# Output products with 32 weight columns instead of 4, and the result stored in two transfers instead of four

## The chip, the cores and the metric

The kernel runs on one core of a Trainium2 chip. The metric is the device time in microseconds (us). The kernel before takes 662.51 us (median of three runs, 662.46 to 662.76).

## The reference

One decoding step of a transformer block for four batch rows of width 640. From the normalised input `xn`, an attention branch over a cache and a gated MLP branch are computed, and both are added to the input:

```python
x = A_x
xn = _layernorm(x, axis=-1)
return x + _A_ref(xn, A_k_cache, A_v_cache, A_wq, A_wo) + _B_ref(xn, B_w_in, B_w_sp, B_b_sp, B_w_out)
```

The attention has 32 heads of 128 elements and 4096 cached positions for each of the four batch rows, one query each. Its two caches are 134 MB each, in bf16:

```python
q = (x @ wq).reshape(B, Sq, Hq, Dh).transpose(0, 2, 1, 3)
scores = jnp.einsum('bhqd,bhkd->bhqk', q, k) * Dh ** (-0.5)
p = _softmax(scores, axis=-1)
o = jnp.einsum('bhqk,bhkd->bhqd', p, v)
return o.transpose(0, 2, 1, 3).reshape(B, Sq, Hq * Dh) @ wo
```

The MLP multiplies `xn` by `w_in` (640 by 1728), applies gelu, normalises one half, scales and shifts it, multiplies it with the other half and multiplies by `w_out` (864 by 640).

## The kernel before

The work is cut into 16 steps: four groups of eight heads, and the four batches of each. A step loads 8 MB of keys into one of two `k_nat` buffers (L139) and 8 MB of values into the single buffer of the pool `vp` (L145); a row of each load is 64 KB in one partition. Nearly all loads are issued by SP, one after the other, in the order that the code gives: MLP and query weights, keys 0 and 1, and from there values and keys by turns. The first tenant of the value buffer is `w_sb`, which holds the MLP weights, and its last is `wo`, the attention's output weights (5.1 MB). These are loaded by four transfers in SP's queue (L159), issued when step 14's values have been used; the last two bring row blocks 11 to 14 and 15 of the second half. The values of step 15 go into a key buffer (`v_last`).

For each step VectorE multiplies the keys by the query (L449), folds the halves (L463), TensorE sums (L475), VectorE reduces (L486) and finds maxima (L495, L505), ScalarE takes the exponentials (L542), VectorE spreads them over the heads (L553), and TensorE weights the values (L568). ScalarE takes the sums out of PSUM (L578), and a small matmul (L591) picks out each head's own row. The schedule is manual: PE, DVE, ACT and SP run in the order in which the code is written; GpSimd (POOL) has constants to make and nothing more (L167 to L176, L232 to L259, L305).

**Output products.** The result is collected in one PSUM tile, `out_ps`, of 128 partitions by 160 columns. `add_out` (L214 to L222) issues four matmuls, one for each quarter q of the 640 output columns; quarter q goes to the partitions from 32q on, in four strips of 32. The moving operand has 160 columns of a weight matrix. The stationary operand holds the four batches, so it has four columns, and the batches stand in lanes 32q to 32q + 3. Only the first call (L224), which adds the input, has 32 columns. There are 12 calls in the MLP, from `yT` (L405) and `yE` (L416), and 32 in the attention (`group_proj`, L653), from two tiles `oT0` and `oT1` of 128 by 16 by 4 that `group_turn` writes (L650, L651): the first half after step 8, the second at the very end. At the end TensorE runs `group_proj(0)`, `group_turn(1)`, `group_proj(1)`; ScalarE copies `out_ps` into `res` (L732); and four transfers of four lanes by 320 bytes each store it (L736), two issued by SP and two by ACT.

Of the kernel before, what the change touches and what calls it, by code (L numbers as in the profile page):

```python
# [10 lines left out]
BF16 = mybir.dt.bfloat16  # L11
ACT = mybir.ActivationFunctionType
ALU = mybir.AluOpType
# [4 lines left out]
def kernel(  # L18
# [39 lines left out]
    GW = P // CG  # L58
    ROWS = HT * Bsz
    NG = 2  # L60
    HP = HG // NG
    WH = NG * HT
    WL = P // WH
    WJ = WH * Dh // P
    WW = 2
    WR = NG * ROWS
    NFF = Fh // P
    TL = 16
    TK = (Fh - NFF * P) // TL
    TE = 4  # L70
    NFC = NFF + TK
    F0 = NFF * P
    TF = TL * TK
    NZ = NFF + 1
    assert F0 + TF == Fh and TF <= P
    NQ = 4
    NO = D // NQ
    REP = GW // Bsz
    assert CB * HT == GW and ROWS == GW

    const = ctx.enter_context(tc.tile_pool(name="const", bufs=1))
    kp = ctx.enter_context(tc.tile_pool(name="kp", bufs=2))
    vp = ctx.enter_context(tc.tile_pool(name="vp", bufs=1))
    work = ctx.enter_context(tc.tile_pool(name="work", bufs=1))
# [12 lines left out]
    def v_slot(name):  # L97
        return vp.tile([P, SLOT], BF16, tag="v", name=name)
# [3 lines left out]
    x_bf = start_t[:Bsz, 0:D]  # L102
# [3 lines left out]
    w_sb = v_slot("w_sb")  # L106
    w_in_sb = w_sb[:, 0 : DC * F].rearrange("p (c n) -> p c n", c=DC)
    w_out_sb = w_sb[:, DC * F : DC * F + NFC * D].rearrange("p (k n) -> p k n", k=NFC)
    nc.sync.dma_start(
        out=w_out_sb[:, 0:NFF, :], in_=B_w_out[0 : NFF * P].rearrange("(p k) n -> p k n", k=NFF)  # L110
    )
# [10 lines left out]
    for l in range(TL // TE):  # L122
        nc.sync.dma_start(
            out=w_out_sb[:TL, NFF:NFC, :].rearrange("(e l) k n -> e l (k n)", e=TE)[:, l],
            in_=B_w_out[F0:Fh].rearrange("(e l k) n -> e l (k n)", e=TE, k=TK)[:, l],
# [25 lines left out]
    wo_t = []  # L151
    WO_CUTS = ((0, WJ), (0, 11, 15, WJ))

    def load_wo():
        t = v_slot("wo")[:, 0 : HP * WJ * D].rearrange("p (g j n) -> p g j n", g=HP, n=D)
        wo_t.append(t)
        for g in range(HP):
            for j0, j1 in zip(WO_CUTS[g], WO_CUTS[g][1:]):
                nc.sync.dma_start(out=t[:, g, j0:j1, :], in_=wo_v[g][:, j0:j1, :])  # L159
# [4 lines left out]
    ident = const.tile([P, P], BF16)  # L164
# [17 lines left out]
    for i in range(NSTAT):  # L182
# [5 lines left out]
        out=rstd[:], in_=mv[:, 1:2], func=ACT.Sqrt, bias=eps_tile[:Bsz], scale=1.0  # L188
# [3 lines left out]
        out=xn_bf,  # L192
        in0=x_bf,
# [8 lines left out]
    for c in range(DC):  # L202
        nc.tensor.transpose(
            out=xnT_ps[:, c, :], in_=xn_v[:, c, :], identity=ident[:Bsz, :Bsz]
# [3 lines left out]
        out=xnT_r[:], in_=xnT_ps[:, :, :, None].to_broadcast([P, DC, Bsz, REP])  # L208
# [5 lines left out]
    def add_out(lhsT, rhs, start=False, stop=False):  # L214
        for q in range(NQ):
            nc.tensor.matmul(  # L216
                out=out_ps[GW * q : GW * q + lhsT.shape[1], :],
                lhsT=lhsT,
                rhs=rhs[:, q * NO : (q + 1) * NO],
                start=start,  # L220
                stop=stop,
            )  # L222

    add_out(ident[:Bsz, :GW], x_bf, start=True)  # L224


    own = const.tile([P, HT], FP32)
# [1 line left out]
        out=own[:], in_=ident_f[:].rearrange("p (h l) -> p h l", h=HT), axis=AX.X, op=ALU.add  # L229
# [4 lines left out]
        out=pick[:, :, GW - HT : GW],  # L234
        in_=ident_f[:].rearrange("p (j h c) -> p c h j", c=CB, h=HT),
        axis=AX.X,
        op=ALU.add,
# [3 lines left out]
        out=row_head_f[:],  # L241
        in_=ident_f[:WR, :WR].rearrange("p (g b h) -> p g h b", g=NG, h=HT),
        axis=AX.X,
        op=ALU.add,
# [3 lines left out]
        out=row_head[:],  # L248
        in_=row_head_f[:].rearrange("p g h -> p (g h)")[:, :, None].to_broadcast([WR, WH, WL]),
# [3 lines left out]
        out=row_batch_f[:],  # L253
        in_=ident_f[:WR, :WR].rearrange("p (g b h) -> p b g h", g=NG, h=HT),
        axis=AX.XY,
        op=ALU.add,
# [10 lines left out]
    for t in range(2):  # L267
        for c in range(DC):
            for j in range(CG):
                n = CG * t + j  # L270
                nc.tensor.matmul(  # L271
                    out=q_ps[t][GW * j : GW * (j + 1), :],
                    lhsT=xnT_r[:, c].rearrange("p b r -> p (b r)"),
                    rhs=wq_t[:, c, n * NW : (n + 1) * NW],
                    start=(c == 0),
# [3 lines left out]
    for t in range(2):  # L279
        qT_ps = ps_m.tile([P, HQ, CG, Bsz, REP], BF16, tag="m", name="qT_ps")  # L280
        for n in range(HQ):
            nc.tensor.transpose(  # L282
                out=qT_ps[:, n].rearrange("p j b r -> p (j b r)"),
                in_=q_rows[:, t, n * Dh : (n + 1) * Dh],
# [3 lines left out]
            out=qT[:, CG * HQ * t : CG * HQ * (t + 1), :].rearrange(  # L288
                "p (j n) b -> p n j b", n=HQ
            ),  # L290
            in_=qT_ps[:, :, :, :, 0],
# [17 lines left out]
    def gmlp():  # L309
        zz, gw, gt, gz, sq = (gm[n] for n in ("zz", "gw", "gt", "gz", "sq"))  # L310
# [30 lines left out]
        for n, src in enumerate((gz[:, 1, :, :], sq)):  # L341
# [51 lines left out]
            out=sq,  # L393
# [7 lines left out]
            in1=ac_sb[:, None, Bsz : 2 * Bsz].to_broadcast([P, NZ, Bsz]),  # L401
            op=ALU.add,
        )
        yT = work.tile([P, NZ, Bsz], BF16, name="yT")
        nc.vector.tensor_tensor(out=yT[:], in0=gz[:, 0, :, :], in1=sq, op=ALU.mult)  # L405
        ye_ps = ps_m.tile([TL, TK, Bsz], FP32, tag="m", name="ye_ps")
        for k in range(TK):
            nc.tensor.matmul(
                out=ye_ps[:, k, :],
                lhsT=ident[:TF, :TF].rearrange("p (f k) -> p k f", k=TK)[:, k, :],  # L410
                rhs=yT[:TF, NFF, :],
                start=True,
                stop=True,
            )
        yE = work.tile([TL, TK, Bsz], BF16, name="yE")
        nc.scalar.copy(out=yE[:], in_=ye_ps[:])  # L416
        for k in range(NFC):
            if k < NFF:
                add_out(yT[:, k], w_out_sb[:, k, :])
            else:  # L420
                add_out(yE[:, k - NFF], w_out_sb[:TL, k, :])


    qbcs, scores, sums_ps, maxes, pms, pvs, es = {}, {}, {}, {}, {}, {}, {}
# [58 lines left out]
    def row_sums(i, u):  # L483
        if u == 0:
            scores[i] = small.tile([P, NC], FP32, name="s_sb", bufs=1)
        nc.vector.tensor_reduce(  # L486
            out=scores[i][:, u * UC : (u + 1) * UC],
            in_=sums_ps[i][:],
            axis=AX.X,
            op=ALU.add,  # L490
        )
# [146 lines left out]
    def group_turn(g):  # L638
        parts = oTs[g]
        JW = WJ // WW  # L640
        t_ps = ps_m.tile([P, WJ, Bsz], FP32, tag="m", name="t_ps")
        for j in range(WJ):
            nc.tensor.matmul(
                out=t_ps[:, j, :],
                lhsT=parts[j // JW][:, j % JW, :, :],
                rhs=row_batch[:],
                start=True,
                stop=True,
            )
        oTs[g] = const.tile([P, WJ, Bsz], BF16, name=f"oT{g}")  # L650
        nc.scalar.copy(out=oTs[g][:], in_=t_ps[:])  # L651

    def group_proj(hg):  # L653
        for j in range(WJ):
            add_out(
                oTs[hg][:, j, :],
                wo_t[0][:, hg, j, :],
                stop=(hg == HP - 1 and j == WJ - 1),
            )
# [14 lines left out]
    with tc.manual_schedule(engines={E.PE, E.DVE, E.Activation, E.SP}):  # L674
        stage_q(0)
        gmlp()
        load_v(0, v_slot("v_nat"))
        for i in range(NT):
            product(i, 0)
            at(i - 1, row_sums, 1)  # L680
            at(i - 1, lane_max)
            at(i - 1, turn_max)
            at(i - 1, head_max)
            at(i - 1, spread_max)
            fold(i, 0)
            joined(i - 2, group_rows)
            sums(i, 0)
            joined(i - 2, group_turn)
            at(i - 1, bias)
            at(i - 1, exps)  # L690
            at(i + 1, stage_q)
            at(i - 1, own_heads)
            at(i - 1, weighted)
            if i == 0:
                pass
            elif i < NT - 1:
                load_v(i, v_slot("v_nat"))
            else:
                load_wo()
            at(i - 1, take)  # L700
            product(i, 1)
            row_sums(i, 0)
            fold(i, 1)
            at(i - 1, diag)
            group(i - 1, group_den)
            sums(i, 1)
            if i + 2 < NT:
                load_k(i + 2)
            elif i + 2 == NT:
                load_v(NT - 1, k_slot("v_last"))  # L710
        L = NT - 1
        row_sums(L, 1)
        lane_max(L)
        joined(L - 1, group_rows)
        turn_max(L)
        head_max(L)
        spread_max(L)
        bias(L)
        exps(L)
        own_heads(L)  # L720
        for c0, c1 in zip(V_CUTS, V_CUTS[1:]):
            weighted(L, c0, c1)
        take(L)
        group_den(HG - 1)
        diag(L)
        group_rows(HP - 1)
        group_proj(0)
        group_turn(HP - 1)
        group_proj(HP - 1)

        res = small.tile([P, NO], BF16, tag="s_sb", name="res", bufs=1)
        nc.scalar.copy(out=res[:], in_=out_ps[:])  # L732
        out_v = out.flatten_outer_dims()
        for q in range(NQ):
            queue = nc.scalar if q % 2 else nc.sync
            queue.dma_start(  # L736
                out=out_v[:, q * NO : (q + 1) * NO], in_=res[GW * q : GW * q + Bsz]
            )


# [28 lines left out]
```

## Time and profile before

| | |
|---|---|
| median of three runs | 662.51 us (662.46 to 662.76) |
| profiled execution, first to last instruction | 661.1 us |
| bytes read | 282.24 MB, 427 GB/s over the span |
| busy: VectorE (DVE) | 491.6 us (74%) |
| busy: TensorE matmul (PE) / weight load (PEld) | 295.4 us (45%) / 127.9 us (19%) |
| busy: ScalarE (ACT) / GpSimd (POOL) | 34.4 us (5%) / 2.1 us |
| granted TensorE clock, mean | 0.712 |

The profile shows one execution. Its time is the span from the first to the last instruction; the runs' time also counts what lies around the span, some 1.4 us here. Engines have the names in brackets, SP issues transfers, and a q behind a name means its instruction queue (ACTq, SPq). A group of instructions is named by its line in the kernel, what it writes and what it reads; "128*4 128x160" is a matmul with 128 rows and 4 weight columns that writes 128 by 160 elements as the profile counts them. An entry "[0.62 <-DMA wo]" says how long the engine had been idle before and what ended it.

### The profile page before, as it was taken

How to read it: one execution, taken by the hardware profiler on the slowest of the kernel's cores; microseconds unless marked ns; L12 is line 12 of the kernel's file. 1: busy time of each engine (PE TensorE's matmuls, PEld its weight loads, DVE VectorE, ACT ScalarE, POOL GpSimd, SP SyncE). 2: the span in 40 equal slices, each digit the busy share in tenths (PEclk: the TensorE clock that was granted, in tenths of full speed). 3: DMA queues.
4: the chain of work that ended last, by engine and by line, in shares of the span. 5: the costliest groups of instructions: out<-in, count | busy, mean ns of one | idle time of the engine just before them, and what ended most of it. 6: DMA issues, size and time to landing. Idle time of an engine off the chain costs nothing.

```text
span 661.1 us, 4720 instructions
## 1 busy us (share of the span) xinstructions
PE 295.4 (45%) x2099; PEld 127.9 (19%) x2099; DVE 491.6 (74%) x222; ACT 34.4 (5%) x94; POOL 2.1 (0%) x15
## 2 busy tenths in 40 slices
PE   0513464536426253552625344362634507263656
PEld 0301121212112021220202112120211202031223
DVE  1249999959597795959779569986959699695851
ACT  0300000000000000000000000000000000000000
POOL 1000000000000000000000000000000000000000
PEclk9756676876858687675868757787775768777688
DMA  8999999999999999999999999999999999999996
GB/s 377 456 428 444 428 417 441 429 436 441 436 420 433 432 429 445 440 421 432 424 436 441 440 425 432 420 441 436 437 428 437 425 432 429 440 432 437 432 406 275
DMA packets 5712, 282.55 MB, mean 427 GB/s; under 512 B 680, under 2 KB 812, under 8 KB 1084
## 3 DMA queue, kind: packets, MB, share of 16 engines
q1 hardware_dynamic: 5664, 282.24, 98.9%
q8 instruction: 16, 0.26, 0.2%
q14 instruction: 4, 0.03, 0.0%
q10 hardware_dynamic: 28, 0.01, 0.0%
HBM read 282.24 MB, written 0.01 MB: 427 GB/s over the span
## 4 chain that ended last, share of the span: by engine, by line
DMA 51%; DVE 37%; PE 9%; issue 2%; ACT 1%; SPq 0%; DVEq 0%; ACTq 0%
DMA k_nat<-in_A_k_cache_dram 47%; DVE k_nat L449 22%; DVE k_nat L463 11%; PE s_ps L475 8%; DMA wo<-in_A_wo_dram 4%; DVE s_sb L486 3%; DMA w_sb<-in_B_w_out_dram 1%; ACT p L542 1%; PE pv L568 1%; DVE m L495 1%; PE mT L500 0%; DVE nm L505 0%; DVE pm L553 0%; SPq L159 0%; PE out_ps L216 0%
## 5 line engine op out<-in xcount | busy, mean ns | idle before, releaser
L449 DVE TENSOR_TENSOR k_nat<-k_nat,qbc 128x16384 bf16<-128x16384 bf16 x32 | 278.0, 8688 | 97.8 <-DMA k_nat<-in_A_k_cache_dram 97.8
L475 PE MATMUL s_ps<-k_nat,ident 128*128 128x512 bf16 x528 | 184.8, 528 | 139.3 <-DVE k_nat L463 139.3
L463 DVE TENSOR_TENSOR k_nat<-k_nat 128x8192 bf16<-128x8192 bf16 x31 | 136.7, 4410 | 0.0
L475 PEld LDWEIGHTS <-ident 128*128 128x128 bf16 x528 | 65.3, 129 | 248.3 <-DVE k_nat L463 123.3
L500 PE MATMUL mT<-ident_f,m 128*1 128x128 f32 x16 | 5.9, 366 | 160.0 <-DVE m L495 160.0
L568 PE MATMUL pv<-v_nat,pm 128*32 128x512 bf16 x960 | 56.1, 387 | 0.8 <-DVE pm L553 0.8
L486 DVE TENSOR_REDUCE s_sb<-s_ps 128x128 f32<-128x1024 f32 x32 | 39.0, 1218 | 5.4 <-PE s_ps L475 5.4
L500 PEld LDWEIGHTS mT<-ident_f,m 128*1 128x1 f32 x16 | 1.3, 79 | 167.8 <-DVE m L495 156.2
L568 PEld LDWEIGHTS <-pm 128*32 128x32 bf16 x1024 | 27.1, 100 | 34.3 <-issue 8.5
L553 DVE TENSOR_TENSOR pm<-p,own_c 128x2048 bf16<-128x2048 bf16 x16 | 19.6, 1225 | 15.3 <-ACT p L542 15.3
L542 ACT ACTIVATE p<-s_sb,nb 128x256 bf16<-128x256 f32 x16 | 8.1, 508 | 394.1 <-DVE nb_h L524 394.1
L591 PE MATMUL o_ps<-e,pick 128*32 128x128 f32 x128 | 17.0, 276 | 11.2 <-ACT e L578 11.2
L591 PEld LDWEIGHTS o_ps<-e,pick 128*32 128x32 f32 x128 | 12.7, 109 | 18.7 <-ACT e L578 18.7
L578 ACT COPY e<-pv 128x512 f32<-128x512 f32 x16 | 9.4, 586 | 68.1 <-PE pv L568 60.6
L287 DVE COPY qT<-qT_ps 128x64 bf16<-128x64 bf16 x2 | 0.4, 224 | 15.5 <-PE qT_ps L282 15.5
L516 PE MATMUL nb_ps<-nm,ones_row 1*128 1x8 f32 x32 | 9.2, 359 | 6.0 <-DVE nm L505 6.0
L505 DVE TENSOR_REDUCE nm<-mT 1x8 f32<-1x128 f32 x16 | 4.5, 279 | 7.5 <-PE mT L500 7.5
L516 PEld LDWEIGHTS nb_ps<-nm,ones_row 1*128 1x128 f32 x32 | 7.7, 298 | 10.6 <-DVE nm L505 9.9
L271 PE MATMUL q_ps<-wq,xnT_r 128*32 128x512 bf16 x40 | 4.3, 609 | 11.2 <-DMA wq<-in_A_wq_dram 11.2
L443 ACT CAST qbc<-qbc_ps 128x128 bf16<-128x128 f32 x16 | 4.3, 266 | 92.3 <-PE qbc_ps L435 92.3
L608 PE MATMUL den<-ones_col,acc_h 128*32 128x1 f32 x8 | 1.0, 194 | 16.6 <-DVE acc_h L601 16.6
L495 DVE TENSOR_REDUCE m<-s_sb 128x1 f32<-128x256 f32 x16 | 6.7, 420 | 0.5
(92 smaller groups left out, 70.7 us busy)
## 6 DMA issues: line engine op xcount, KB each, us to landing
wq<-in_A_wq_dram SPq DMA_DIRECT2D x1, 5120.0 KB, 16.3
wo<-in_A_wo_dram SPq DMA_DIRECT2D x1, 2560.0 KB
w_sb<-in_B_w_in_dram SPq DMA_DIRECT2D x1, 2160.0 KB, 20.9
wo<-in_A_wo_dram SPq DMA_DIRECT2D x1, 1760.0 KB
w_sb<-in_B_w_out_dram SPq DMA_DIRECT2D x1, 960.0 KB
wo<-in_A_wo_dram SPq DMA_DIRECT2D x1, 640.0 KB, 25.5
k_nat<-in_A_k_cache_dram SPq DMA_DIRECT2D x16, 39.6
v_nat<-in_A_v_cache_dram SPq DMA_DIRECT2D x15, 33.7
```

Source lines behind the costliest of these rows:

```text
L449: nc.vector.tensor_tensor(out=part(i, u), in0=part(i, u), in1=qbcs[i][:, None, :].to_broadcast([P, UC, Dh]), op=ALU.mult,)
L463: nc.vector.tensor_tensor(out=t[:, :, 0:HD2], in0=t[:, :, 0:HD2], in1=t[:, :, HD2:Dh], op=ALU.add)
L475: nc.tensor.matmul(out=sums_ps[i][:, c : c + SC], lhsT=ident[:], rhs=t[:, c : c + SC, g * RW : (g + 1) * RW], start=(g == 0), stop=(g == n ...
L486: nc.vector.tensor_reduce(out=scores[i][:, u * UC : (u + 1) * UC], in_=sums_ps[i][:], axis=AX.X, op=ALU.add,)
L495: nc.vector.tensor_reduce(out=m1[:], in_=scores[i][:], axis=AX.X, op=ALU.max)
L500: nc.tensor.transpose(out=mT[:], in_=maxes[i][:], identity=ident_f[:])
L516: nc.tensor.matmul(out=nb_ps[:], lhsT=ones_row[:], rhs=maxes[i][:], start=True, stop=True)
L542: nc.scalar.activation(out=probs[i][:], in_=scores.pop(i)[:], func=ACT.Exp, bias=maxes.pop(i)[:], scale=scale_qk, accum_out=accs[hg][:, b ...
L553: nc.vector.tensor_tensor(out=pm[:], in0=probs.pop(i)[:] .rearrange("p (n c) -> p n c", c=CB)[:, :, None, :] .to_broadcast([P, NB, HT, CB] ...
L568: nc.tensor.matmul(out=pvs[i][j * GW : (j + 1) * GW, :], lhsT=pm[:, n, :, :].rearrange("p h c -> p (h c)"), rhs=v_nat[:, n * CB : (n + 1) ...
L578: nc.scalar.copy(out=es[i][:], in_=pvs.pop(i)[:].rearrange("p (c d) -> p c d", d=Dh))
L591: nc.tensor.matmul(out=o_ps[hg // NG][own_rows(hg), :], lhsT=pick[:, c, GW - HT - HT * b : 2 * GW - HT - HT * b], rhs=e[:, c, :], start=(b ...
```

## The change

The stationary operand of every output product gets 32 columns: batch b stands in column 8b (`REP` is 8), and the seven columns behind it are zero. So the results stand in lanes 32q + 8b, and each of the two transfers at the end takes the eight lanes of two quarters, one issued by ACT and one by SP. Three places provide the zeroed room. `x_rep` is a new constant of four by 32 elements. `y_rep` lies behind the MLP weights in `w_sb`; `o_rep` lies behind the output weights in `wo`, 1024 elements a partition. GpSimd zeroes both. The results are then written into every eighth column: `yT` by VectorE, `yE` by ScalarE, the second half of the attention by ScalarE straight from PSUM. The first half still goes to `oT0` after step 8, since the room in `wo` isn't there yet, and a new copy, `group_rep`, brings it over after the last turn of the loop, ahead of the last step's exponentials on ACT.

```diff
+    y_at = DC * F + NFC * D
+    y_rep = w_sb[:, y_at : y_at + (NZ + TK) * GW].rearrange(
+        "p (k b r) -> p k b r", b=Bsz, r=REP
+    )
+    yT, yE = y_rep[:, 0:NZ], y_rep[:TL, NZ : NZ + TK]
...
     def load_wo():
-        t = v_slot("wo")[:, 0 : HP * WJ * D].rearrange("p (g j n) -> p g j n", g=HP, n=D)
+        w = v_slot("wo")
+        t = w[:, 0 : HP * WJ * D].rearrange("p (g j n) -> p g j n", g=HP, n=D)
         wo_t.append(t)
+        o_rep = w[:, HP * WJ * D : HP * WJ * (D + GW)]
+        nc.gpsimd.memset(o_rep, 0.0)
+        wo_t.append(o_rep.rearrange("p (g j b r) -> p g j b r", g=HP, b=Bsz, r=REP))
...
-    add_out(ident[:Bsz, :GW], x_bf, start=True)
+    x_rep = const.tile([Bsz, Bsz, REP], BF16)
+    nc.gpsimd.tensor_copy(
+        out=x_rep[:], in_=ident[:Bsz, :Bsz, None].to_broadcast([Bsz, Bsz, REP])
+    )
+    nc.gpsimd.memset(w_sb[:, y_at : y_at + (NZ + TK) * GW], 0.0)
+    add_out(x_rep[:].rearrange("c b r -> c (b r)"), x_bf, start=True)
...
-        yT = work.tile([P, NZ, Bsz], BF16, name="yT")
-        nc.vector.tensor_tensor(out=yT[:], in0=gz[:, 0, :, :], in1=sq, op=ALU.mult)
+        nc.vector.tensor_tensor(
+            out=yT[:, :, :, 0], in0=gz[:, 0, :, :], in1=sq, op=ALU.mult
+        )
...
-        yE = work.tile([TL, TK, Bsz], BF16, name="yE")
-        nc.scalar.copy(out=yE[:], in_=ye_ps[:])
+        nc.scalar.copy(out=yE[:, :, :, 0], in_=ye_ps[:])
...
-                add_out(yT[:, k], w_out_sb[:, k, :])
+                add_out(yT[:, k].rearrange("p b r -> p (b r)"), w_out_sb[:, k, :])
...
-        oTs[g] = const.tile([P, WJ, Bsz], BF16, name=f"oT{g}")
-        nc.scalar.copy(out=oTs[g][:], in_=t_ps[:])
+        if g == HP - 1:
+            nc.scalar.copy(out=wo_t[1][:, g, :, :, 0], in_=t_ps[:])
+        else:
+            oTs[g] = const.tile([P, WJ, Bsz], BF16, name=f"oT{g}")
+            nc.scalar.copy(out=oTs[g][:], in_=t_ps[:])
+
+    def group_rep(g):
+        nc.scalar.copy(out=wo_t[1][:, g, :, :, 0], in_=oTs[g][:])
...
-                oTs[hg][:, j, :],
+                wo_t[1][:, hg, j].rearrange("p b r -> p (b r)"),
...
         L = NT - 1
+        for g in range(HP - 1):
+            group_rep(g)
         row_sums(L, 1)
...
-        out_v = out.flatten_outer_dims()
-        for q in range(NQ):
-            queue = nc.scalar if q % 2 else nc.sync
+        out_v = out.flatten_outer_dims().rearrange("b (q n) -> q b n", n=NO)
+        QH = NQ // 2
+        for h, queue in enumerate((nc.scalar, nc.sync)):
             queue.dma_start(
-                out=out_v[:, q * NO : (q + 1) * NO], in_=res[GW * q : GW * q + Bsz]
+                out=out_v[QH * h : QH * (h + 1)],
+                in_=res[GW * QH * h : GW * QH * (h + 1) : REP],
             )
```

More of the change, by code (lines that the diff above doesn't have):

```diff
@@ L410, in gmlp @@
                 lhsT=ident[:TF, :TF].rearrange("p (f k) -> p k f", k=TK)[:, k, :],
-                rhs=yT[:TF, NFF, :],
+                rhs=yT[:TF, NFF, :, 0],
                 start=True,
@@ L414, in gmlp @@
             )
-        yE = work.tile([TL, TK, Bsz], BF16, name="yE")
-        nc.scalar.copy(out=yE[:], in_=ye_ps[:])
+        nc.scalar.copy(out=yE[:, :, :, 0], in_=ye_ps[:])
         for k in range(NFC):
             if k < NFF:
-                add_out(yT[:, k], w_out_sb[:, k, :])
+                add_out(yT[:, k].rearrange("p b r -> p (b r)"), w_out_sb[:, k, :])
             else:
-                add_out(yE[:, k - NFF], w_out_sb[:TL, k, :])
+                add_out(yE[:, k - NFF].rearrange("p b r -> p (b r)"), w_out_sb[:TL, k, :])
     qbcs, scores, sums_ps, maxes, pms, pvs, es = {}, {}, {}, {}, {}, {}, {}
```

## The prediction

> **What bounds the kernel now.** I read the page's transfer rows first, then the busy times by stretches, then the last microseconds in the timeline.
>
> ```profile
> DMA  8999999999999999999999999999999999999996
> q1 hardware_dynamic: 5664, 282.24, 98.9%
> ```
>
> The 16 transfer engines are full from the first slice to the last but one. SP's queue q1 moves 282.24 MB in 98.9% of the engines' span, 0.989 x 661.1 = 653.8 us. No engine row comes near: VectorE has 74%. So a step in the middle is paid for only if it delays the issue of a transfer so long that the queue runs dry, and the question is what happens ahead of the stream, inside it and behind it.
>
> ```profile
> core 0: us, PE busy (x) PEld busy (x) DVE busy (x) ACT busy (x) POOL busy (x), PEclk, DMA share, GB/s
> 20.00:40.00 20.00, 9.30 (x159) 6.86 (x151) 4.04 (x23) 5.25 (x11) 0.00 (x0) 0.62 1.04 449
> 40.00:60.00 20.00, 3.56 (x9) 1.38 (x10) 16.73 (x3) 0.00 (x0) 0.00 (x0) 0.50 1.01 436
> ...
> 620.00:630.00 10.00, 10.00 (x81) 4.35 (x83) 10.00 (x3) 0.00 (x0) 0.00 (x0) 0.89 1.04 452
> ```
>
> The last two columns are the share and the rate of the transfers (packets are counted where they fall, so a share can pass 1). Rate over share is 449/1.04 = 432, 436/1.01 = 432 and 452/1.04 = 435 GB/s.
>
> ```profile
> 643.04 0.51 ACT L542 ACTIVATE p<-s_sb,nb 128x256 bf16<-128x256 f32 x1 [11.49 <-DVE nb_h L524]
> ...
> 644.95 0.10 PEld L568 LDWEIGHTS <-pm 128*32 128x32 bf16 x1 [2.31 <-DVE pm L553]
> 645.39 5.64 PE L568 MATMUL pv<-v_last,pm 128*32 128x512 bf16 x64 [2.65 <-DMA v_last<-in_A_v_cache_dram]
> ...
> 655.71 0.93 PE L216 MATMUL out_ps<-wo,oT 128*4 128x160 bf16 x44 [0.32 <-DMA wo<-in_A_wo_dram]
> 657.27 0.64 PE L216 MATMUL out_ps<-wo,oT 128*4 128x160 bf16 x20 [0.62 <-DMA wo<-in_A_wo_dram]
> ...
> 658.01 0.29 ACT L732 CAST res<-out_ps 128x160 bf16<-128x160 f32 x1 [2.38 <-PE out_ps L216]
> 658.33 0.64 SPq L736 DMA_DIRECT2D out_dram<-res  x2
> 658.34 0.62 ACTq L736 DMA_DIRECT2D out_dram<-res  x2
> ```
>
> The end hangs on the stream too: TensorE waits for `v_last` until 645.39, though its weights were ready at 644.95 (0.44 us of slack), and for `wo` until 657.27, though its 44 products were done at 655.71 + 0.93 = 656.64 (0.63 us more). What follows is serial: 20 products, the copy to `res`, the issue of the stores, their landing.
>
> **The change part by part.**
>
> *Setting up.* GpSimd gets `x_rep` and a memset of 416 elements.
>
> ```profile
> 0.87 0.10 POOL L169 MEMSET eps_tile<- 128x1 f32 x1
> ...
> 1.41 0.28 POOL L176 MEMSET pick<- 128x224 f32 x1
> 1.63 0.28 POOL L167 CAST ident_f<-ident 128x128 f32<-128x128 bf16 x1
> ...
> 6.01 0.32 PE L216 MATMUL out_ps<-start_t,ident 4*32 4x160 bf16 x4
> ...
> 6.69 0.21 POOL L232 CAST own_c<-own 128x32 bf16<-128x32 f32 x1 [4.78 <-DVE own L228]
> ```
>
> A memset costs 0.10 us and (0.28 - 0.10)/223 = 0.8 ns an element, so some 0.43 us, and `x_rep` about the 0.21 us of `own_c`. Both fit into GpSimd's 4.78 idle us from 1.91 on; the product that reads `x_rep` stands at 6.01. Cost: 0; without that cover it would still be 0, since TensorE's next wait is for `wq` at 17.51. No transfer moves: SP's waits up to keys 1 don't name GpSimd.
>
> *MLP.* 48 products (24 and 24) get 32 columns, and `yT` and `yE` are written eight elements apart; the writes also wait for the memset, long past. The work runs from 33.38 to 35.7; behind it stands the load of values 0, the last tenant change of `w_sb`.
>
> ```profile
> 35.70 0.33 SPq L145 DMA_DIRECT2D v_nat<-in_A_v_cache_dram  x1
> ...
> v_nat<-in_A_v_cache_dram SPq DMA_DIRECT2D x1, 46.2
> ```
>
> This load lands 46.2 us after its issue, because the two key loads ahead of it keep the queue full. A delay of even 1 us is hidden; uncovered, it would shift the stream by its length.
>
> *The zeroed room in `wo`.* GpSimd's memset of 1024 elements costs 0.10 + 0.8 = 0.95 us. It must wait until step 14's values are used, as the `wo` load does; the load's own place in SP's queue and its two waits stay, and it doesn't wait for the memset (other bytes of the tile).
>
> ```profile
> 630.15 4.42 DVE L463 TENSOR_TENSOR k_nat<-k_nat 128x8192 bf16<-128x8192 bf16 x1
> 630.90 1.75 SPq L159 DMA_DIRECT2D wo<-in_A_wo_dram  x4
> 630.97 0.59 ACT L578 COPY e<-pv 128x512 f32<-128x512 f32 x1 [11.72 <-PE pv L568]
> ...
> 655.43 0.21 ACT L651 CAST oT<-t_ps 128x64 bf16<-128x64 f32 x1 [3.71 <-PE t_ps L643]
> ```
>
> So it stands at about 630.9 to 631.9, beside VectorE's fold. No row shows the two engines in each other's way there; if the fold lost the whole 0.95 us, the slack of 0.44 + 0.63 = 1.07 us would take it, so 0 at either bound.
>
> *The copy of the first half* on ACT (0.21 us by L651) follows the copy at 630.97 and the memset: done near 632.2. Behind it in ACT's queue is only the exponential of 643.04, after 11.49 idle us. Cost 0, with 10.8 us to spare.
>
> *The end.* The first 108 of the 128 attention products lie ahead of the wait at 657.27. What weights of 32 columns cost:
>
> ```profile
> L216 PEld LDWEIGHTS <-oT x128: 80/81/85, 652.2 to 657.7; 128*4 128x4 bf16 x128
> L216 PE MATMUL out_ps<-wo,oT x128: 229/232/233, 652.2 to 657.7; 128*4 128x160 bf16 x128
> ...
> L216 PEld LDWEIGHTS <-ident x4: 94/96/97, 6.0 to 6.0; 4*32 4x32 bf16 x4
> ...
> L568 PEld LDWEIGHTS <-pm x128: 92/97/150, 627.2 to 650.4; 128*32 128x32 bf16 x128
> ```
>
> A load of 32 columns takes 96 or 97 ns, one of four 81: 16 ns more. The four strips' loads lie beside each other and beside the running products (at 6.0 us four loads of 95 ns and four products of 310 end within 0.33 us), so I take 16 ns once, +0.02 us, nearest to that row. The bounds are 0 and 16 ns for each of the 20, +0.32 us. The Trainium skill, "TensorE: Matmul & The Clock Gate", section "LDWEIGHTS (loading the stationary operand)", speaks against the change: it gives columns/1.2 ns, an estimate of 27 ns against 3, so +0.48 us if 20 loads ran one by one. By that the sum below would be nearly 0; the trace has the growth at 16 ns, not 23.
>
> The stores are where something goes.
>
> ```profile
> L736 SPq DMA_DIRECT2D out_dram<-res x2: 280/290/300, 658.3 to 658.7; - x2
> L736 ACTq DMA_DIRECT2D out_dram<-res x2: 271/290/308, 658.3 to 658.6; - x2
> ...
> L764 SPq EVENT_SEMAPHORE  x7: 17/28/990, 659.0 to 661.0; - x7
> ...
> SPq L764 <- DMA out_dram<-res: 1.0, 1, 1.0
> ```
>
> Each queue issues two stores, 0.29 us apiece. SP's second ends at 658.33 + 0.64 = 658.97, and SP then waits 0.99 us for them before the kernel's closing steps, which end at 661.1. With one store a queue, the last issue is over 0.34 us sooner (0.64 - 0.30), and the landing moves with it if eight lanes travel as four do. For the price of eight lanes I have the issue of `x`, four lanes of 1280 bytes:
>
> ```profile
> L104 ACTq DMA_DIRECT2D start_t<-in_A_x_dram x1: 554/554/554, 0.7 to 0.7; - x1
> ```
>
> so between 0 and 0.55 - 0.30 = +0.25 us; I take +0.03, near the stores' own rows, as the bytes are few. SP's closing list of waits has the stores' counters near its front now and at its back afterwards; at a few such waits of 0.03 us and their gaps this is worth up to -0.15 us, and I take -0.05.
>
> *Addresses.* A constant of 128 bytes a partition goes (`oT1`) and one of 64 comes (`x_rep`), so the key and value buffers move by 64 bytes. I take 0: no row shows a buffer at another place, and the windows from 20 to 60 us, the first with some shorter rows in it, give the same 432 GB/s.
>
> **Sum:** -0.34 + 0.03 - 0.05 + 0.02 = -0.34 us. The profiled span goes from 661.1 to 660.8 us, and the median, 1.4 us above it, from 662.51 to **662.2 us**, -0.05%. I call a difference under 0.2% (1.3 us) no change: that is about what a measurement of this kernel can tell from none.
>
> **The rivals.**
>
> *The loads slow the last products.* For it: the loads are longer. Against: four strips at once. 662.2 + 0.3 = 662.5 us, still no change.
>
> *The buffers' new place changes the stream's rate.* A row that begins off a memory boundary may cost a piece more at its ends; with 64 bytes less, rows may begin on one. For it: 98.9% of the time is in this stream, and one window had 435 where the others have 432 GB/s. Against: the shares are rounded to a hundredth, and 432 stands in both windows from 20 to 60 us. At 435 throughout, 653.8 x 3/435 = 4.5 us would go: 657.7 us. Named beside it: the Trainium skill, "DMA: Bandwidth & Descriptors", section "How a descriptor splits into AXI transactions", says that a piece must start on a 256-byte address and that the bytes before it are paid for. By its table two beats in 2050 would go for a 64-KB row, an estimate of 0.6 us, to 661.6.
>
> *Slower: the new copy blocks ACT.* It stands ahead of step 15's exponential and reads nothing of `wo`, but writes a tile that four transfers fill. Were it held until these have landed (after 657.27), everything from 643.04 on would follow: 657.5 instead of 643.04 is +14.5 us, less the waits for transfers that vanish (0.44 + 0.63), +13.4: 675.9 us. It decides from 643 us on; a copy done before costs nothing. Against: the counts that it waits for in the built program are those of the loads before `wo`, all landed by 630.9, and the memset.
>
> **How the numbers follow.** Forecast 662.2 us with chance 0.65; the loads' rival 0.07 (both within 0.2%); the stream 0.08 to the faster side and 0.04 to the slower (+4.5 us); the blocked copy 0.05. Another 0.11 I leave to what the trace doesn't show, 0.07 of it to the faster side. Faster by over 0.2%: 0.15; within: 0.72; slower: 0.13. The range runs from the end's best (-0.34 - 0.15, less the last digit of 98.9%, 0.1% of 653.8 or 0.65, for a slightly better stream: 661.4) to its worst (no gain at the stores, 0.32 for the loads, and the runs' own 0.25: 663.1).
>
> **What would show it.** In the changed profile: two issues at the end, not four, and SP's closing wait over some 0.3 us earlier relative to the copy to `res`; the last 20 products in 0.64 to 0.66 us; loads of 97 ns in place of 81; ACT's new copy near 632 us; q1 at the same 653.8 us. I am wrong if q1's time moves by over 1 us, if the last exponential starts later than 644 us, or if the products at the end take 0.9 us or more.

## The result and the profile after

| | before | after |
|---|---|---|
| median | 662.58 us (21 runs, 662.39 to 663.04) | 661.66 us (21 runs, 661.37 to 662.23) |
| ratio | 1 | 0.9986, 95% interval 0.998 to 0.9993 |
| profiled span | 661.1 us | 659.8 us |

The change takes 0.92 us off, 0.14%. A ratio of 1 lies outside the interval, but the difference stays inside the 0.2% that the prediction called no change. The time lies in the range given (661.4 to 663.1), 0.5 us below the forecast of 662.2. The cause is not the one forecast, as the traces show first and the runs then settle.

The timed execution with a span of 659.8 us took 661.68 us. So some 1.8 us lie around the span, not the 1.4 that the prediction got from a span and a median of different executions. A run of the kernel before with a listed span has as much (662.57 us for a span of 660.8), so it falls out of the difference. By this 1.8 us the profiled execution of the kernel before took about 662.9 us (an estimate), 0.3 us above the median. So the two spans differ by more than the medians do, 1.3 against 0.92 us.

The page of the changed kernel, span, transfer row and queue rows:

```profile
span 659.8 us, 4735 instructions
DMA  9999999999999999999999999999999999999996
q1 hardware_dynamic: 5658, 282.24, 98.9%
```

The stream has the same bytes and the same share, of a shorter span: 0.989 x 659.8 = 652.5 us instead of 653.8. That would be 1.3 us, and the prediction named over 1 us as a sign that it was wrong. But a share rounded to a tenth of a per cent is good to some 0.3 us only. The durations of the queue's transfer records, added up and divided by 16 engines, are 653.63 and 652.74 us: 0.89 us apart, just short of that sign. Where the time goes is seen along the timeline. The keys' product of step 9 (steps count from 0) starts when its keys have landed; first before, then after (columns: start, duration, engine and line, and the idle time before it with what ended it):

```profile
373.11 8.69 DVE L449 TENSOR_TENSOR k_nat<-k_nat,qbc 128x16384 bf16<-128x16384 bf16 x1 [6.69 <-DMA k_nat<-in_A_k_cache_dram]
```

```profile
372.36 8.69 DVE L463 TENSOR_TENSOR k_nat<-k_nat,qbc 128x16384 bf16<-128x16384 bf16 x1 [6.67 <-DMA k_nat<-in_A_k_cache_dram]
```

Half way through, far from any instruction of the attention that the diff touches, the changed kernel is 0.75 us ahead. It is 0.03 ahead at 43.2 us and 0.24 at 140.9 (140.88 against 140.64): the lead grows with the bytes that have passed. So the stream as a whole runs faster. The trace's transfer records say the same: the mean of its 4096 rows of 64 KB is 2424.2 ns before and 2420.7 ns after. One of the 16 transfer engines has 256 of these rows, and 256 x 3.5 ns = 0.90 us. That is not the whole lead of this profile: from the start of the first of these rows to the end of the last it is 622.99 us before and 621.47 after, 1.5 us less. The records don't tell which engine carried which row, so the other 0.6 us are not accounted for.

The changed kernel's last stretch in the timeline:

```profile
629.82 0.95 POOL L164 MEMSET wo<- 128x1024 bf16 x1 [621.70 <-PE pv L582]
...
630.80 0.48 ACT L671 COPY wo<-oT 128x64 bf16<-128x64 bf16 x1 [0.42 <-POOL wo L164]
...
639.85 0.51 ACT L556 ACTIVATE p<-s_sb,nb 128x256 bf16<-128x256 f32 x1 [8.57 <-DVE nb_h L538]
...
643.78 6.03 PE L582 MATMUL pv<-v_last,pm 128*32 128x512 bf16 x64 [4.24 <-DMA v_last<-in_A_v_cache_dram]
...
654.20 0.44 ACT L665 CAST wo<-t_ps 128x64 bf16<-128x64 f32 x1 [3.70 <-PE t_ps L657]
...
654.69 1.75 PE L225 MATMUL out_ps<-wo 128*32 128x160 bf16 x64 [0.53 <-ACT wo L665]
656.54 0.29 ACT L754 CAST res<-out_ps 128x160 bf16<-128x160 f32 x1 [1.90 <-PE out_ps L225]
656.86 0.60 SPq L758 DMA_DIRECT2D out_dram<-res  x1
656.87 0.64 ACTq L758 DMA_DIRECT2D out_dram<-res  x1
```

`v_last` lands at 643.78 instead of 645.39. The last 64 products now run in one piece behind ACT's write (L665) and wait for `wo` no more. Two things at the end are dearer than the kernel before had them. ACT's write into every eighth element takes 0.44 us, where the plain one (L651) took 0.21. And the single store of each queue takes 0.60 and 0.64 us to issue, about as long as the two it replaces. From the start of the copy to `res` to the end of the span it is 659.8 - 656.54 = 3.26 us, against 661.1 - 658.01 = 3.09 before: the end got longer by 0.17 us, where the prediction had it 0.36 shorter.

So two theories stand against each other. **Address**: one constant of 128 bytes went and one of 64 came, which moved the key and value buffers from byte 20032 of each partition (64 past a multiple of 256) to 19968 (a multiple of 256), each 64-KB row is written a little faster for that, and the rest of the change gains nothing. **Stores**: the merged stores and the new end bring the gain, and the stream's lead is the chance of one profile. What the stores themselves cost, and whether the lane step or the number of issues sets it, is the second question.

### The profile page after: what moved, and what is told of

Same layout as the page of the kernel before. It is cut to its first block, busy times and chain, and to the rows that moved or that the text cites. A ratio compares the mean times of both kernels' runs of the same rounds, so it can differ in the third digit from the quotient of the medians.

```text
span 659.8 us, 4735 instructions
## 1 busy us (share of the span) xinstructions
PE 293.0 (44%) x2099; PEld 127.5 (19%) x2099; DVE 491.7 (75%) x222; ACT 35.1 (5%) x95; POOL 3.5 (1%) x18
## 3 DMA queue, kind: packets, MB, share of 16 engines
q1 hardware_dynamic: 5658, 282.24, 98.9%
## 4 chain that ended last, share of the span: by engine, by line
DMA 49%; DVE 40%; PE 8%; issue 2%; ACT 1%; DVEq 0%; SPq 0%; ACTq 0%
DMA k_nat<-in_A_k_cache_dram 42%; DVE k_nat L463 24%; DVE k_nat L477 12%; DMA v_last<-in_A_v_cache_dram 6%; PE s_ps L489 6%; DVE s_sb L500 3%; PE pv L582 1%; ACT p L556 1%; DMA w_sb<-in_B_w_out_dram 1%; DVE m L509 1%; PE mT L514 0%; DVE nm L519 0%; PE out_ps L225 0%; PE o_ps L605 0%; PE den L622 0%
## 5 line engine op out<-in xcount | busy, mean ns | idle before, releaser
L489 PE MATMUL s_ps<-k_nat,ident 128*128 128x512 bf16 x528 | 182.5, 523 | 140.3 <-DVE k_nat L477 140.3
L582 PE MATMUL pv<-v_last,pm 128*32 128x512 bf16 x64 | 6.0, 559 | 4.2 <-DMA v_last<-in_A_v_cache_dram 4.2
```

The source lines that it names most:

```text
L489: nc.tensor.matmul(out=sums_ps[i][:, c : c + SC], lhsT=ident[:], rhs=t[:, c : c + SC, g * RW : (g + 1) * RW], start=(g == 0), stop=(g == n ...
L582: nc.tensor.matmul(out=pvs[i][j * GW : (j + 1) * GW, :], lhsT=pm[:, n, :, :].rearrange("p h c -> p (h c)"), rhs=v_nat[:, n * CB : (n + 1) ...
```

## The experiments

Each gives its median, and its ratio to the kernel before on the same chip (662.56, 662.67 and 662.62 us in the three groups) with its 95% interval. These intervals reach 0.5 to 0.7 us to each side of the estimate in most runs, so a difference of 0.2 us between two kernels is told from zero only where a profile's rows show it too.

**1. `before_pad192`: the address alone.** The kernel before with 192 unused bytes, so that its buffers start on a multiple of 256 too.

```diff
+    const.tile([P, 96], BF16, name="pad")
     pick = const.tile([P, CB, 2 * GW - HT], FP32)
```

> The kernel before with an unused constant of 192 bytes a partition, so that the key and value buffers begin on a multiple of 256 bytes instead of 64 past one. Prediction (addresses cost nothing, the stores carry the gain): 662.6 us, q1 busy 653.8 us. Address theory (a row that begins off the boundary costs a piece more): about 661.4 us, 0.8 to 1.4 below the kernel before, with nothing else of the change in it, and q1 busy near 652.5 us. Chance theory (the two profiles differ by random stalls of the stream): 662.6 us.

661.51 us, ratio 0.9985 (0.9976 to 0.9994). The old kernel, with nothing changed but an address, is 1.05 us faster. The same key product in its timeline:

```profile
372.22 8.69 DVE L450 TENSOR_TENSOR k_nat<-k_nat,qbc 128x16384 bf16<-128x16384 bf16 x1 [6.60 <-DMA k_nat<-in_A_k_cache_dram]
```

It starts 0.89 us earlier than in the kernel before, and the 64-KB rows take 2420.6 ns. Its end, for the comparisons below:

```profile
655.62 0.63 PE L217 MATMUL out_ps<-wo,oT 128*4 128x160 bf16 x20 [0.53 <-DMA wo<-in_A_wo_dram]
...
656.36 0.29 ACT L733 CAST res<-out_ps 128x160 bf16<-128x160 f32 x1 [2.26 <-PE out_ps L217]
```

**2. `after_pad64`: the change without the address.** The changed kernel with 64 unused bytes, which put the buffers back to 64 past.

```diff
+    const.tile([P, 32], BF16, name="pad")
     pick = const.tile([P, CB, 2 * GW - HT], FP32)
```

> The changed kernel with an unused constant of 64 bytes, so that its buffers begin where those of the kernel before do. Prediction: 661.7 us, as without it. Address theory: the gain goes, 662.6 to 663.0 us, and step 15's values land about 1.5 us later, near 645.4 us. Chance theory: 661.7 us.

662.81 us, ratio 1.0003 (0.9994 to 1.0012). The gain is gone, and the stream's lead with it (rows of 2424.2 ns):

```profile
373.10 8.69 DVE L464 TENSOR_TENSOR k_nat<-k_nat,qbc 128x16384 bf16<-128x16384 bf16 x1 [6.68 <-DMA k_nat<-in_A_k_cache_dram]
```

Its end shows the forecast order of things, with the two waits for `wo` back:

```profile
655.48 0.95 PE L226 MATMUL out_ps<-wo 128*32 128x160 bf16 x44 [0.84 <-DMA wo<-in_A_wo_dram]
...
657.04 0.67 PE L226 MATMUL out_ps<-wo 128*32 128x160 bf16 x20 [0.61 <-DMA wo<-in_A_wo_dram]
...
657.81 0.29 ACT L755 CAST res<-out_ps 128x160 bf16<-128x160 f32 x1 [2.69 <-PE out_ps L226]
658.13 0.60 SPq L759 DMA_DIRECT2D out_dram<-res  x1
```

The last 20 products take 0.67 us instead of 0.64: 32 columns cost 0.03 us here, as the prediction had it (0.02). With the result above, these two runs make a square: off the boundary 662.56 us before and 662.81 changed; on it 661.51 and 661.66. Each column falls by about 1.1 us with the address, and each row rises by 0.15 to 0.25 us with the change proper. Stores, as the source of the gain, falls. The rise is smaller than the intervals, so by times alone a change proper that costs nothing isn't excluded.

**3. `before_pad64`, `before_pad160`, `before_pad224`: how far past.** The pad of experiment 1 with 32, 80 and 112 elements puts the buffers 128, 224 and 32 bytes past a multiple of 256. The question is whether the cost grows with the distance or is one for every place off the boundary.

```diff
-    const.tile([P, 96], BF16, name="pad")
+    const.tile([P, 32], BF16, name="pad")
```

> The kernel before with an unused constant of 64 bytes: buffers begin 128 bytes past a multiple of 256. Prediction: 662.6 us. Address theory with a cost in proportion to the bytes past the boundary (twice that at 64): 663.2 us, and q1 busy near 654.4 us. Address theory with one fixed cost off the boundary: 662.6 us.

> The kernel before with its buffers 224 bytes past a multiple of 256 (it has 64 by itself). One fixed cost off the boundary: 662.6 us, as at 64 and 128. A cost that grows with the bytes past the boundary, which the runs at 64 and 128 speak against: above 664 us.

> The kernel before with its buffers 32 bytes past a multiple of 256. One cost off the boundary, whatever the distance: 662.6 us. A cost that grows with the bytes past the boundary: between 661.5 (at 0) and 662.6 us (at 64), near 662.0 us.

| bytes past 256 | kernel | median, us | ratio (interval) | mean 64-KB row, ns |
|---|---|---|---|---|
| 0 | `before_pad192` | 661.51 | 0.9985 (0.9976 to 0.9994) | 2420.6 |
| 32 | `before_pad224` | 663.0 | 1.0021 (0.9993 to 1.0048) | 2424.7 |
| 64 | before | 662.56 | 1 | 2424.2 |
| 128 | `before_pad64` | 662.59 | 1.0001 (0.9993 to 1.001) | 2423.8 |
| 224 | `before_pad160` | 662.99 | 0.9996 (0.9971 to 1.0021) | 2425.0 |

There is one cheap place, and the cost of the others doesn't grow with the distance. The ratios at 32 and 224, with their wide intervals, settle nothing; these two kernels are read by their rows. Nor is it the chance of single profiles: of all the profiles of this study, the nine with their buffers on the boundary have a median 64-KB row of 2418 ns, and the five off it 2420 or 2421 ns. With the few rows over 2440 ns left out, the mean is 2418.3 to 2418.5 ns in those nine. It is 2421.2 or 2421.3 in the three profiles at 64 and 128 bytes past, and 2422.3 or 2422.4 at 32 and 224, the two distances that aren't multiples of 64. The two medians of 663 us point the same way, but lie within the intervals. A multiple of 512 isn't needed: the first row's buffers start at 20224 (79 x 256), the changed kernel's at 19968 (39 x 512), and both are on the cheap side. The Trainium skill, "DMA: Bandwidth & Descriptors", section "How a descriptor splits into AXI transactions", says that a piece starts on a 256-byte address and the bytes before it are paid for. The traces agree that 256 is the boundary. By its table a 64-KB row would have 1, 2, 4 and 7 beats more in 2048 at 32, 64, 128 and 224 past, an estimate of 0.3 to 2.2 us for the stream; the rows here lie within 1.2 ns of each other, so that growth doesn't show.

**4. `after_four`: the change with four stores.** Lanes still eight apart, but four stores of four lanes, to price the merging.

```diff
-        out_v = out.flatten_outer_dims().rearrange("b (q n) -> q b n", n=NO)
-        QH = NQ // 2
-        for h, queue in enumerate((nc.scalar, nc.sync)):
+        out_v = out.flatten_outer_dims()
+        for q in range(NQ):
+            queue = nc.scalar if q % 2 else nc.sync
             queue.dma_start(
-                out=out_v[QH * h : QH * (h + 1)],
-                in_=res[GW * QH * h : GW * QH * (h + 1) : REP],
+                out=out_v[:, q * NO : (q + 1) * NO],
+                in_=res[GW * q : GW * (q + 1) : REP],
             )
```

> The changed kernel with four stores of four lanes, two from each queue, as before, from lanes eight apart. Prediction: the stores' gain goes, 662.0 us. Address theory with stores that cost instead of saving: 661.4 us, 0.2 to 0.3 below the changed kernel; the copy to res to the end of the span takes 3.05 us instead of 3.24.

662.40 us, ratio 0.9997 (0.9989 to 1.0006), 0.76 us more than the changed kernel (each taken against its own before: -0.16 and -0.92). Neither number on record came (662.0 and 661.4): both took four-lane stores from lanes eight apart to be as cheap as plain ones. Its store rows (shortest, middle and longest ns of one issue, then the first and last start):

```profile
L758 SPq DMA_DIRECT2D out_dram<-res x2: 608/627/646, 656.8 to 657.5; - x2
L758 ACTq DMA_DIRECT2D out_dram<-res x2: 706/742/779, 656.8 to 657.5; - x2
```

So merging does save most of a microsecond, but against stores that the lane step has made dear first: 0.61 to 0.78 us apiece, where the kernel before has 0.27 to 0.31 for the same four lanes and bytes.

**5. `after_contig8`: is it the lane step?** The two merged stores, but from eight neighbouring lanes (of the eight lanes only the first holds a batch, so most of the output is not the result).

```diff
-                in_=res[GW * QH * h : GW * QH * (h + 1) : REP],
+                in_=res[GW * QH * h : GW * QH * h + QH * Bsz],
```

> The changed kernel, but its two stores take eight neighbouring lanes each (0 to 7 and 64 to 71) instead of every eighth one; these lanes don't hold the result, so part of the output is left out and the time alone counts. Theory that the step between lanes doubles the cost of an issue: 0.30 us an issue instead of 0.60 to 0.64, 661.2 to 661.4 us. Theory that eight lanes, or two dimensions of them, cost it: 0.60 us an issue still, 661.7 us.

661.73 us, ratio 0.9985 (0.9976 to 0.9994), no different from the changed kernel. The issues stay at 0.69 (SP) and 0.74 us (ACT):

```profile
L758 SPq DMA_DIRECT2D out_dram<-res x1: 692/692/692, 657.0 to 657.0; - x1
L758 ACTq DMA_DIRECT2D out_dram<-res x1: 735/735/735, 657.0 to 657.0; - x1
```

So the lane step alone is not the cause: a store from neighbouring lanes is dear as well while its destination has two dimensions, as merging makes it (two quarters of each of four rows).

**6. `after_first4`: 32 columns, batches side by side.** The zeroed room, the copies and the 32-column weights stay, but the batches stand in the first four columns instead of every eighth. So ACT's writes and the four stores are plain again. The buffers stay on the boundary.

```diff
-        "p (k b r) -> p k b r", b=Bsz, r=REP
+        "p (k r b) -> p k b r", b=Bsz, r=REP
...
-        wo_t.append(o_rep.rearrange("p (g j b r) -> p g j b r", g=HP, b=Bsz, r=REP))
+        wo_t.append(o_rep.rearrange("p (g j r b) -> p g j b r", g=HP, b=Bsz, r=REP))
...
+    const.tile([P, 32], BF16, name="pad")
...
-    add_out(x_rep[:].rearrange("c b r -> c (b r)"), x_bf, start=True)
+    add_out(ident[:Bsz, :GW], x_bf, start=True)
...
-                out=out_v[QH * h : QH * (h + 1)],
-                in_=res[GW * QH * h : GW * QH * (h + 1) : REP],
+                out=out_v[:, q * NO : (q + 1) * NO], in_=res[GW * q : GW * q + Bsz]
```

> The changed kernel with its 32 weight columns, but the batches in the first four of them and four stores of four neighbouring lanes as before; an unused constant of 64 bytes keeps the buffers where they are. What is left of the change is the 32 columns, the zeroing and the copy of the first half. Prediction (0.02 us for the loads): as the kernel before on aligned buffers, 661.5 us. Rival that the loads slow the last products: 661.8 us or more. Step theory: issues of 0.30 us, and 0.9 us below the version with four stores of lanes eight apart (662.40 us).

661.37 us, ratio 0.9982 (0.9973 to 0.9991), beside 0.9985 for `before_pad192`, which has none of this. So 32 columns, the zeroing and the extra copy cost nothing that can be measured. Of the changed kernel's parts only the lane step and the merging are left. Its end:

```profile
653.78 0.21 ACT L662 CAST wo<-t_ps 128x64 bf16<-128x64 f32 x1 [3.70 <-PE t_ps L654]
...
655.92 0.64 PE L226 MATMUL out_ps<-wo 128*32 128x160 bf16 x20 [0.57 <-DMA wo<-in_A_wo_dram]
...
656.66 0.29 ACT L751 CAST res<-out_ps 128x160 bf16<-128x160 f32 x1 [2.67 <-PE out_ps L226]
656.98 0.65 SPq L755 DMA_DIRECT2D out_dram<-res  x2
```

ACT's write is back at 0.21 us and two issues of SP take 0.65 together.

**7. `halves_pad192`: two plain stores in another way.** The kernel before on the boundary with two column strips instead of four (`NQ = 2`): the products write 320 columns each, and each queue has one store of four neighbouring lanes.

```diff
-    NQ = 4
+    NQ = 2
...
+    const.tile([P, 96], BF16, name="pad")
...
-        nc.scalar.copy(out=res[:], in_=out_ps[:])
+        nc.scalar.copy(out=res[: GW * NQ], in_=out_ps[: GW * NQ])
```

> The kernel before on buffers that begin on a multiple of 256 bytes, with the output in two halves of 320 columns instead of four quarters of 160: two products a call, and two stores of four neighbouring lanes by 640 bytes, one a queue. Step theory: each issue 0.30 us, so the second issue's 0.35 us go; the products cost 0.1 to 0.3 us more behind the last transfer and the copy to res 0.13 us. 661.1 to 661.6 us, against 661.51 in quarters.

661.37 us, ratio 0.9982 (0.9973 to 0.9991). Its end:

```profile
654.23 2.36 PE L217 MATMUL out_ps<-wo,oT 128*4 128x320 bf16 x32 [0.49 <-DMA wo<-in_A_wo_dram]
656.68 0.42 ACT L733 CAST res<-out_ps 64x320 bf16<-64x320 f32 x1 [2.70 <-PE out_ps L217]
657.13 0.29 SPq L737 DMA_DIRECT2D out_dram<-res  x1
657.13 0.28 ACTq L737 DMA_DIRECT2D out_dram<-res  x1
```

A store of twice the bytes a lane issues in 0.28 or 0.29 us, like the small ones. From the copy to the end of the span it is 659.4 - 656.68 = 2.72 us, 0.32 less than the 3.04 of `before_pad192`, though the copy takes 0.13 longer. The prediction's 0.34 for a second issue is there, where the stores are plain. The products give it back: the copy starts at 656.68 instead of 656.36.

**8. `store_step8` and `store_step2`: the lane step alone.** `before_pad192` with its four stores taking every eighth or every second lane (three of the four rows stored are then not the results).

The edit for step 8; for step 2 the last part is `res[GW * q : GW * q + 2 * Bsz : 2]`:

```diff
-                out=out_v[:, q * NO : (q + 1) * NO], in_=res[GW * q : GW * q + Bsz]
+                out=out_v[:, q * NO : (q + 1) * NO], in_=res[GW * q : GW * (q + 1) : REP]
```

> The kernel before on aligned buffers (661.51 us) with one thing more: its four stores read every eighth lane of a strip instead of four neighbours. The lanes don't hold the result, so part of the output is left out. Theory that a step between the lanes makes an issue dear: 0.6 to 0.8 us an issue, 662.2 to 662.5 us. Theory that the dear issues come from the changed products ahead of them: 0.30 us, 661.5 us.

> The same with every second lane; part of the output is left out. If any step costs: as with a step of eight. If it is the width of the step: between 661.5 and 662.4 us.

Step 8: 662.24 us, ratio 0.9995 (0.9985 to 1.0004), 0.67 above `before_pad192` (-0.38 against -1.05, each from its own before). Step 2: 662.55 us, 0.9999 (0.999 to 1.0008). First step 8, then step 2:

```profile
L737 SPq DMA_DIRECT2D out_dram<-res x2: 602/620/638, 656.7 to 657.4; - x2
```

```profile
L737 SPq DMA_DIRECT2D out_dram<-res x2: 597/618/638, 657.5 to 658.2; - x2
```

The issue of a four-lane store goes from 290 to 620 ns whether the step is 2 or 8, and on ACT from 290 to 736 ns. So either step doubles it or more. In the profile of step 2 `wo` landed some 0.7 us later, which the stores have no part in. The stream itself was slower there: the product of step 9 starts at 372.87 us, 0.65 later than in `before_pad192` with its buffers in the same place, and the 64-KB rows have a mean of 2423.0 ns, though a median of 2418. This was the longest of the ten runs (663.09 us). The 0.3 us between the medians of the two steps stays unexplained.

**9. `store_eight_rows`: two merged stores with neither step nor second dimension.** `before_pad192` with two stores of eight neighbouring lanes to eight neighbouring pieces of 320 bytes. The lanes don't hold the results; it prices the best that merging could be.

```diff
-        out_v = out.flatten_outer_dims()
-        for q in range(NQ):
-            queue = nc.scalar if q % 2 else nc.sync
+        out_v = out.flatten_outer_dims().rearrange("b (q n) -> (b q) n", n=NO)
+        QH = 2 * Bsz
+        for h, queue in enumerate((nc.scalar, nc.sync)):
             queue.dma_start(
-                out=out_v[:, q * NO : (q + 1) * NO], in_=res[GW * q : GW * q + Bsz]
+                out=out_v[QH * h : QH * (h + 1)], in_=res[GW * 2 * h : GW * 2 * h + QH]
             )
```

> The kernel before on aligned buffers with two stores of eight neighbouring lanes, each to eight neighbouring pieces of 320 bytes of the output, so that neither side has a second dimension; the lanes don't hold the result, so part of the output is left out. Theory that two dimensions cost the time in the stores of eight neighbouring lanes (0.69 and 0.74 us an issue): 0.30 us, 661.1 to 661.3 us. Theory that the eight lanes cost it: 0.7 us, 661.5 to 661.7 us.

660.74 us, ratio 0.997 (0.9959 to 0.9981): the fastest of all, 0.83 below `before_pad192` (-1.88 against -1.05).

```profile
L737 SPq DMA_DIRECT2D out_dram<-res x1: 317/317/317, 656.8 to 656.8; - x1
L737 ACTq DMA_DIRECT2D out_dram<-res x1: 298/298/298, 656.8 to 656.8; - x1
```

Eight plain lanes issue in 0.30 to 0.32 us, as four do. From the copy to the end of the span it is 659.1 - 656.51 = 2.59 us, 0.45 less than in `before_pad192`. That the median gains more than the profile's end (0.83) lies within the two intervals.

The ends side by side, from the start of the copy to `res` to the end of the span of each profile:

| stores | kernel | us |
|---|---|---|
| four plain | before / `before_pad192` / `after_first4` | 3.09 / 3.04 / 3.04 |
| two, step 8 and two dimensions | after / `after_pad64` | 3.26 / 3.19 |
| two, two dimensions, no step | `after_contig8` | 3.29 |
| four, a step | `after_four` / `store_step8` / `store_step2` | 4.01 / 4.09 / 4.06 |
| two plain, four lanes (copy 0.13 longer) | `halves_pad192` | 2.72 |
| two plain, eight lanes | `store_eight_rows` | 2.59 |

Of the versions that store the kernel's whole result, `after_first4` and `halves_pad192` have the lowest medians, 661.37 us, and `before_pad192`, one line away from the kernel before, has 661.51. The changed kernel's 661.66 is not told apart from them.

## Why the prediction was right in its number and wrong in its reason

**Stores, -0.34 + 0.03: wrong.** The step that failed is the price of a store of eight lanes. The prediction bounded what eight lanes add by 0 and 0.25 us and took 0.03, the end nearest to the stores' own rows. Its arithmetic was that one issue instead of two is 0.34 us sooner. The second issue did go, but the remaining one takes 0.605 and 0.642 us instead of 0.29, so ACT's ends 0.97 us after the copy began (656.87 + 0.64 - 656.54) and the slower queue's was at 0.96 (658.33 + 0.64 - 658.01) before. It wasn't the number of lanes: eight plain ones take 0.30 to 0.32 us (experiment 9). It was the shape: a step between lanes (8), or a destination of two dimensions (5), doubles an issue. Where the merged stores were plain, the saving was there, 0.45 us from the copy to the end (experiment 9). No row of the trace before had a store of the changed shape, and the upper bound that the prediction did have, `x` with 0.55 us, was the nearer one.

**Order of SP's closing waits, -0.05: not seen.** SP's own wait for the stores grew, 1.0 us before and this after (waits of SP's queue; total, times, longest):

```profile
SPq L787 <- DMA out_dram<-res: 1.2, 1, 1.2
```

Behind the last issue the rest of the span takes 659.8 - 657.51 = 2.29 us against 661.1 - 658.97 = 2.13. So the three terms of the end, together -0.36, measured +0.17.

**Addresses, "I take 0": wrong, and this decides.** It is worth -1.05 us (-0.0015, interval -0.0024 to -0.0006) by `before_pad192`. The rival with this mechanism was named and given 0.08. Its price from the rows, 4.5 us, was far too large: it rested on 435 against 432 GB/s, rates from a share rounded to a hundredth, as the prediction itself held against it. The estimate beside it by the table of the Trainium skill, "DMA: Bandwidth & Descriptors", section "How a descriptor splits into AXI transactions", 0.6 us, lies within the interval (0.4 to 1.6 us), though the dependence on the distance that it implies was not found. The argument against it, 432 GB/s in two windows, couldn't see the effect: 3.5 ns in 2424 is 0.14%, and a rate read to a hundredth of a share is good to 1%.

**Loads of 32 columns, +0.02: right.** 97 ns instead of 81 (as given), +0.03 us on the last 20 products in `after_pad64`, and no cost in `after_first4`. This row is of the changed kernel:

```profile
L225 PEld LDWEIGHTS <-wo x128: 92/97/151, 651.0 to 656.0; 128*32 128x32 bf16 x128
```

**Setting up, MLP, zeroed room, 0: right.** The memset in `wo` took 0.951 us at 629.82 (0.95 forecast; the forecast's own terms, 0.10 us and 0.8 ns for each of 1024 elements, add up to 0.92), beside VectorE's fold, which kept its 4.42 us; the one in `w_sb` took 0.434 us (0.43). Behind the MLP the load of values 0 was issued 0.18 us later (35.88 us against 35.70), and the transfers queued ahead of it hid that, as forecast.

**The copy of the first half on ACT, 0: right in its place, dearer than forecast.** It ran from 630.80, long before the exponential, so the rival that it blocks ACT didn't happen. It took 0.48 us and not 0.21, with its elements eight apart (0.24 us in `after_first4`, where four stand side by side), and it was hidden.

**Not foreseen: the same strided write where nothing hides it.** L665 stands on the serial end and takes 0.23 us more than L651. Off the boundary it is covered by the wait for `wo`, as in `after_pad64`. In the changed kernel's own profile, on the boundary, `wo` has come early enough that this chain bounds the end: the copy to `res` starts at 656.54 against 656.36 in `before_pad192`, which still waits for `wo` until 655.62.

The sum of -0.34 and the measured -0.92 thus have the same sign for unlike reasons: -1.05 from the stream, +0.13 left over for everything that the change was described by (-0.92 + 1.05), to which the strided write and the stores fit by their rows, though by times alone 0.13 us is not told from zero. That the sign came right was luck. So was it that 661.66 us lies in the range: its lower end held 0.65 us for a slightly better stream, taken from the last digit of the 98.9% and not from the address. Without it the range would have ended at 662.0 us.

Three points stay open: why a step or a second dimension doubles an issue; why an unaligned start costs a row about as much at 32 bytes past (4.1 ns) as at 224 (4.4 ns); and why the landings gain more than the rows' mean accounts for. No run here takes them apart further.

## What to carry to other kernels

In a kernel bound by one stream of transfers, an edit that adds or drops a small constant can move every large buffer: look up where the buffers start before and after, and put them on a multiple of 256 bytes before judging the edit by its time. Here the address was worth 0.15%, as much as the whole edit seemed to be. Price a transfer's issue by a row of the same shape, with its lane step and the dimensions of both its sides; a count of issues alone misleads. To find which of two effects won, build the two corners that the diff doesn't have, the edit without the shift and the shift without the edit.

## What the runs showed of the hardware that was not expected

- A 64-KB row from DRAM into SBUF took 2420.6 to 2421.6 ns in the mean with its buffer on a multiple of 256 bytes (2423.0 in one of nine profiles), and 2423.8 to 2425.0 ns at 32, 64, 128 and 224 bytes past one.
- A store's issue took 0.27 to 0.32 us for four or eight neighbouring lanes of 320 or 640 bytes, and 0.60 to 0.78 us with a step of 2 or 8 lanes or a destination of two dimensions.
- ACT wrote 64 elements a partition from PSUM in 0.21 us side by side and in 0.44 us eight apart.
